# Part A's last projection chunk with high and low weights in one array, and a new split of the maxima over the projection products

## The chip, the cores and the metric

The kernel runs on one core of one Trainium2 chip. The metric is the device time of one execution in microseconds; lower is better. The core's engines work side by side, each through its own list of instructions in order, and wait for each other through semaphores: TensorE (PE, with its weight loads as PEld), VectorE (DVE), ScalarE (ACT), GpSimd (POOL), and SyncE (SP), which here only issues DMA transfers.

## What is computed

Two attention blocks over x of 2048 rows and 576 columns, 32 heads of 18. Part A is local and dilated, part B is full. Their outputs stand side by side.

```python
# part A
qkv = (x @ wqkv).reshape(B, S, 3, H, Dh)...
idx = pos[:, None] - off[None, :]          # 8 keys, 2 apart
kg = k[:, :, idx_c, :]; vg = v[:, :, idx_c, :]
attn = softmax(where(mask, einsum("bhsd,bhswd->bhsw", q, kg) * scale, -1e9))
a = einsum("bhsw,bhswd->bhsd", attn, vg)... @ wo
# part B
scores = einsum("bhqd,bhkd->bhqk", q, k) * scale
b = einsum("bhqk,bhkd->bhqd", softmax(scores), v)... @ wo
return concatenate([a, b], axis=-1)
```

## The kernel before

Every float32 operand of a projection is split into a high part (rounded to TensorE's fp32r) and a low part (the rest), and a product is the sum of three: high by high, high by low, low by high. The 576 input rows are four pieces of 128 and a last one of 64, whose high and low parts of x share one tile (`xhl`) on the two halves of the partitions, so that it takes two passes in place of three.

**Start.** Three chunks of part B's q and k (`w0`) and half of its values are projected with full 128-row passes.

**The stream** (function `stream`, passes recorded at L491) follows: 96 products in groups of four. A product is cut into two halves by rows of the weights' contraction: half 0 on partitions 0 to 63, half 1 on 64 to 127, which run side by side on the array. A turn j takes half 0 of one product and half 1 of another, so that a group takes four turns and both halves of a product add up in the same PSUM bank; 13 or 14 passes a half, 27 a product (`halves`, with the triples from `pairs`). The products are 16 of the other values (288 columns wide), 24 of part B's q and k (`w1`, `w2`) and 56 of part A: 14 chunks of its 1728 columns, 13 of 128 columns and the last, number 13, of 64, each for four blocks of 512 rows of x. In a group, product k has bank k of the ring "scores" (banks 0 to 3).

Among the passes stand **maxima** of part B's scores: `maximum(r)` multiplies 128 queries with 512 keys on half r (L239) into one of three banks (ring "else", banks 4 to 6), and DVE reduces it (L256, L258). A pair is one on each half. The function handed to `stream` as `most` says how many pairs have been given by each turn; by the end it is `EARLY_PAIRS`, 264. The last turn also holds the four scores of the first step of the main loop (`others`; L388), which ACT turns into exponentials (L398).

After the third and the fourth turn of a group its products are emptied (`leave_a` for part A): ACT copies a bank into one of the four buffers `ohi` (L819), and SP stores it to the array `da` in DRAM (L820). The product that stands second in number is copied first. In the 64-column chunk the copy and the store have 64 partitions.

The weights of a part A chunk come in `chunk`: `put` and `put_last` have ACT make the high part and POOL the low part (L538, L539), as tiles `ahi`, `alo` (four pieces) and `ahh`, `all` (the last piece). `a_room` deals the chunks out to pools in turn, one buffer each.

**The main loop** has 511 steps over 8 groups of heads, 4 blocks of queries and 16 of keys: four scores, their exponentials, products with v (L870), and the maxima of blocks two groups ahead; part A's local attention runs on POOL beside it from step 10 on, and reads `da`: q and k before, v 16 steps later. Its first step begins with half of a two-part maximum in bank 0, a score in bank 1 and a whole maximum in bank 2 (`PLAIN`, "D1AzwE2B"); the pair tile for `z` and `w` is banks 5 and 6, and the score `2` goes to bank 3.

Nothing reorders the work at run time: the order of every engine is what the program records, and the functions above set it.

Of the kernel before, what the change touches and what calls it, by code (L numbers as in the profile page):

```python
# [23 lines left out]
NT = S // 128  # L24
# [16 lines left out]
EARLY_PAIRS = EARLY * NB * PIECES + 8  # L41
# [28 lines left out]
def two_attentions(ctx: ExitStack, tc, xa, wa, woa, xb, wb, wob, out):  # L70
# [5 lines left out]
    nc = tc.nc  # L76
# [354 lines left out]
    def halves(r, odd, w, x, wcols, xcols, weights_move=False):  # L431

        at = slice(64 * r, 64 * r + 64)
        both = [p for c in range(4) for p in pairs(c, w, x, wcols, xcols)] + pairs(4, w, x, wcols, xcols)[: 1 + (r == odd)]
        return [(b[at], a[at]) if weights_move else (a[at], b[at]) for a, b in both]


    ctx.enter_context(tc.manual_schedule())
    make_set(stack0, 0)
# [11 lines left out]
    def stream(products, most, last):  # L451

        where, ends = {}, {}  # L460
        for j in range(len(products)):
            first = j - j % 4
            turn = [((0, 0), (1, 1)), ((0, 2), (1, 3)), ((0, 1), (1, 0)), ((0, 3), (1, 2))][j % 4]
            both = []
            for r, k in turn:
                args, view, _ = products[first + k]
                if j % 4 < 2:
                    where[k] = view(bank("scores"))
                else:
                    assert int(sum(given)) - ends[k] > 3  # L470
                parts = halves(r, *args)
                both.append([(where[k], *ab, j % 4 < 2 and i == 0, j % 4 > 1 and i == len(parts) - 1)
                             for i, ab in enumerate(parts)])
            n = most(j) - given[0]
            others = last if j == len(products) - 1 else ([], [])
            n += len(others[0])
            total = n + len(both[0])
            for r in range(2):
                for i in range(n):
                    both[r].insert((4 * i + 1 + 2 * r) * total // (4 * n), None)  # L480
            narrow = where[turn[0][1]].shape[-1] < 512
            spent = [0, 0]
            while any(both):
                r = int(not both[0] or bool(both[1]) and spent[1] < spent[0])
                p = both[r].pop(0)
                spent[r] += 133 if p and narrow else 226
                if p is None:
                    (others[r].pop(0) if others[r] else maximum(r))()
                else:
                    ps, a, b, start, stop = p  # L490
                    nc.tensor.matmul(ps, a, b, start=start, stop=stop)  # L491
            for _, k in turn:
                if j % 4 < 2:
                    ends[k] = int(sum(given))
                else:
                    products[first + k][2](where[k])
            slot()
# [5 lines left out]
    every = slice(0, 512)  # L503
# [4 lines left out]
    with (tc.tile_pool(name="x", bufs=1, side="right") as xp,  # L508
# [28 lines left out]
        def split(engine, hi, lo, t):  # L537
            nc.scalar.activation(hi, t, AF.Copy)  # L538
            engine.tensor_sub(lo, t, hi)  # L539
# [38 lines left out]
        def chunk(c):  # L578

            n = min(128, 3 * D - 128 * c)  # L580
            t = {}
            w = [None] * 4

            def get():
                t[0] = rp.tile([128, 512], F32, name="raw", bufs=5)
                load(ap(t[0], (n, 4), (1, n)), rows(wa[0, 128 * c], (3 * D, 128), (128 * 3 * D, 4), (1, n)))

            def get_last():
                t[1] = rp.tile([128, 512], F32, name="raw", bufs=5)
                for r in range(2):  # L590
                    load(t[1][64 * r : 64 * r + 64, :n], wa[512:, 128 * c : 128 * c + n])

            def put():
                hi, lo = (a_room(c).tile([128, 512], F32R, name=nm, bufs=1) for nm in ("ahi", "alo"))
                split(nc.gpsimd, hi[:, : 4 * n], lo[:, : 4 * n], t[0][:, : 4 * n])
                w[:2] = ([u[:, n * k : n * k + n] for k in range(4)] for u in (hi, lo))

            def put_last():
                w[2:] = (a_room(c).tile([128, 128], F32R, name=nm, bufs=1) for nm in ("ahh", "all"))
                split(nc.gpsimd, w[2][:, :n], w[3][:, :n], t[1][:, :n])  # L600

            return w, [get, get_last], [put, put_last]

        def a_room(c):
            return a0 if c % 2 == 0 else a1 if c == 1 else wp


        qkv, odd = ExitStack(), ExitStack()
# [3 lines left out]
        if True:  # L612
# [34 lines left out]
            for c in range(5):  # L647
                one, other = (load, nc.scalar.dma_start) if c % 2 == 0 else (nc.scalar.dma_start, load)
# [9 lines left out]
            x = [t[0] for t in xs]  # L658
# [69 lines left out]
            for t in range(NT):  # L728
                ps = bank()
# [10 lines left out]
            xas = [inputs(xa, b, nc.gpsimd, spare="more" if b == NB - 1 else False) for b in range(NB)]  # L740
            w1, w1_get, w1_put = weights(proj[1], wb, turn_cols(1), nc.vector)
            w2, w2_get, w2_put = weights(proj[0], wb, turn_cols(2), nc.gpsimd)
            ws = [chunk(c) for c in range(14)]

            def second_rows():

# [61 lines left out]
            for k in range(2, 14):  # L808
                n = 46 if k == 2 else 36 + 4 * k
# [6 lines left out]

            def leave_a(c, b, n, ps):
                o = xp.tile([128, 512], F32, name="ohi", bufs=4)
                nc.scalar.activation(o[:n], ps, AF.Copy)  # L819
                load(da[128 * c : 128 * c + n, HALO + 512 * b : HALO + 512 * b + 512], o[:n])  # L820


            order = [t for i in (0, 8) for j in range(4) for t in (i + j, i + j + 4)]
            ring = "else"
            nc.vector.memset(po, 0.0)
            work_list = []
# [12 lines left out]
            for c, b in order:  # L839
                n = min(128, 3 * D - 128 * c)  # L840
                work_list.append(((b % 2, ws[c][0], xas[b][0], slice(0, n), every),
                                  lambda ps, n=n: ps[:n], lambda ps, c=c, b=b, n=n: leave_a(c, b, n, ps)))

            es = []
            few = 6 * NT // 4
            turns = len(work_list) - NT
            stream(work_list, lambda j: 6 * (j // 4) + (1, 3, 5, 6)[j % 4] if j < NT else
                   few + (EARLY_PAIRS - few) * (j - NT + 1) // turns,
                   [[lambda h=h: es.append(score(0, 0, 0, h, "apart" if h in (1, 2) else "single")) for h in (r, r + 2)] for r in range(2)])
        wa_room.close()  # L850

# [304 lines left out]
    turns = []  # L1156
# [200 lines left out]
    while step < ALL:  # L1357
        n, kt = divmod(step, NT)
        g, b = divmod(n, NB)
# [4 lines left out]
        products = inside.pop(0)() if inside else ([], [])  # L1364
# [3 lines left out]
        parts = many == 3 or many == 1 and open_parts  # L1368
# [75 lines left out]
```

## Time and profile before

| | us |
|---|---|
| median of 3 runs | 1590.14 |
| lowest, highest | 1588.71, 1592.66 |
| profiled execution, its own time | 1589.66 |
| its span, first to last instruction | 1587.8 |
| value products of the stream | 74.6 to 109.7 |
| part B's other products of the stream | 109.7 to 201.3 |
| part A's products, 128 columns | 201.3 to 400.5 |
| part A's products, 64 columns | 400.5 to 417 |
| main loop's first wait on the stream is over | 418.5 |

The profile is one execution seen by the hardware profiler. A row of the timeline has the start in us from the span's start, the time it covers, engine, line, operation, the tile written and those read, the shape (rows\*columns of the weights for a pass, then what is streamed) and a count; in brackets the engine's idle time before it and what ended that. A row of a group has the count, busy us and mean ns of one, and the idle time before. A pass of 64 rows lasts some 390 ns from its start to its modelled end, but passes overlap, so what a pass costs is read from the starts of those that follow.

### The profile page before, as it was taken

What the parts mean: (1) busy time and instruction counts of PE and PEld (TensorE: products, weight loads), DVE (VectorE), ACT (ScalarE), POOL (GpSimd) and SP (SyncE); (2) the same over time, 40 slices, a digit from 0 to 9 for tenths busy, and PEclk for the clock granted to TensorE, in tenths of its full rate; (3) what the DMA queues carried; (4) which work ended last, traced back from release to release, by engine and by line L of the source; (5) the groups of instructions that cost most, each with busy time, mean ns of one, the idle gap of its engine ahead of it and who ended that gap; (6) DMA issues with size and microseconds to landing.
All of it is one profiled execution on the core that took longest, in us unless ns stands there. A gap on an engine that the chain in (4) does not pass through costs nothing.

```text
span 1587.8 us, 34762 instructions
## 1 busy us (share of the span) xinstructions
PE 1577.4 (99%) x13436; PEld 971.1 (61%) x13436; DVE 1399.7 (88%) x2381; ACT 1180.6 (74%) x1912; POOL 961.6 (61%) x816
## 2 busy tenths in 40 slices
PE   9999999999999999999999999999999999999998
PEld 7999999999544444444444445444445445455776
DVE  5299999999999999999998999999999999999433
ACT  6324441121699999999998999999999999998444
POOL 2305752201157997994994995995995997940100
PEclk9999999999999999999999999999999999999999
DMA  9848954532322253253236225324613232234211
GB/s 258 222 142 207 274 171 124 146 98 76 75 52 58 63 115 90 69 127 113 60 83 167 52 76 134 104 50 107 143 53 91 70 87 78 61 125 157 85 39 60
DMA packets 190149, 173.12 MB, mean 109 GB/s; under 512 B 123120, under 2 KB 136944, under 8 KB 188256
## 3 DMA queue, kind: packets, MB, share of 16 engines
q1 hardware_dynamic: 185120, 159.36, 36.1%
q0 software_dynamic: 4032, 10.63, 3.2%
q8 instruction: 105, 1.72, 0.5%
q10 hardware_dynamic: 832, 0.92, 0.2%
q14 instruction: 60, 0.49, 0.1%
HBM read 97.47 MB, written 72.95 MB: 107 GB/s over the span
## 4 chain that ended last, share of the span: by engine, by line
PE 97%; DVE 2%; DMA 1%; issue 0%; ACT 0%; POOL 0%; SPq 0%; ACTq 0%; DVEq 0%; POOLq 0%
PE po L870 31%; PE bank L239 20%; PE bank L491 17%; PE bank L388 10%; PE bank L1211 8%; PE pair L388 7%; PE bank L424 4%; DVE mx L256 1%; DMA at<-dao 0%; DVE mx L272 0%; DVE o L880 0%; PE bank L643 0%; DVE mx L258 0%; DMA out<-y 0%; PE bank L1189 0%
## 5 line engine op out<-in xcount | busy, mean ns | idle before, releaser
L239 PE MATMUL bank<-ks,qs 54*128 54x256 f32 (+1 forms) x2526 | 754.6, 372 | 1.0 <-ACT ohi L819 0.9
L256 DVE TENSOR_REDUCE mx<-bank 128x1 f32<-128x512 f32 x1024 | 680.1, 684 | 63.8 <-PE bank L239 39.6
L239 PEld LDWEIGHTS bank<-ks,qs 54*128 54x128 f32 x2526 | 414.2, 184 | 424.3 <-DVE mx L272 305.0
L398 ACT ACTIVATE e<-bank 128x512 f32<-128x512 f32 x1024 | 610.1, 602 | 71.5 <-PE bank L388 64.4
L870 PE MATMUL po<-ee,v 128*19 128x512 f32 x2048 | 537.1, 599 | 1.0 <-DVE o L880 0.2
L870 PE MATMUL po<-e,v 128*19 128x512 f32 x2048 | 531.8, 599 | 0.0
L401 ACT ACTIVATE ee<-pair 128x1024 f32<-128x1024 f32 x478 | 487.2, 1019 | 0.9 <-PE pair L388 0.3
L388 PE MATMUL bank<-qs,ks 56*128 56x512 f32 x1092 | 461.0, 442 | 0.0
L258 DVE TENSOR_REDUCE mx<-bank 128x2 f32<-128x512 f32 x546 | 356.5, 684 | 19.5 <-PE bank L239 6.6
L272 DVE TENSOR_REDUCE mx<-bank 128x2 f32<-128x512 f32 x478 | 326.1, 682 | 0.0
L388 PE MATMUL pair<-qs,ks 56*128 56x512 f32 x956 | 248.7, 396 | 0.0
L388 PEld LDWEIGHTS bank<-qs,ks 56*128 56x128 f32 x1092 | 194.6, 184 | 15.9 <-ACT e L398 9.0
L1062 POOL TENSOR_TENSOR pr<-lg,akv 128x1024 f32<-128x1024 f32 x72 | 157.0, 2200 | 0.6
L819 ACT ACTIVATE ohi<-bank 128x512 f32<-128x512 f32 (+1 forms) x56 | 30.4, 595 | 156.4 <-issue 129.1
L388 PEld LDWEIGHTS pair<-qs,ks 56*128 56x128 f32 x956 | 138.1, 185 | 0.1
L870 PEld LDWEIGHTS po<-ee,v 128*19 128x19 f32 x2048 | 69.6, 96 | 112.0 <-issue 108.1
L491 PE MATMUL bank<-xhi,ahi 64*128 64x512 f32 (+1 forms) x448 | 120.2, 390 | 0.0
L491 PE MATMUL bank<-xhi,alo 64*128 64x512 f32 (+1 forms) x448 | 114.5, 390 | 0.0
L491 PE MATMUL bank<-xlo,ahi 64*128 64x512 f32 (+1 forms) x448 | 108.8, 391 | 0.1
L1014 POOL TENSOR_TENSOR pr<-aq,akv 128x1024 f32<-128x1024 f32 x40 | 87.8, 2202 | 18.3 <-PE bank L239 17.1
L1064 POOL TENSOR_TENSOR pr<-pr 128x512 f32<-128x512 f32 x72 | 91.1, 1285 | 0.6
L539 POOL TENSOR_TENSOR alo<-raw,ahi 128x512 fp32r<-128x512 f32 (+1 forms) x14 | 17.6, 1257 | 117.4 <-ACT ahi L538 86.0
(206 smaller groups left out, 2383.7 us busy)
## 6 DMA issues: line engine op xcount, KB each, us to landing
do<-n SPq DMA_DIRECT2D x28, 512.0 KB
da<-ohi SPq DMA_DIRECT2D x52, 256.0 KB
akv<-da SPq DMA_DIRECT2D x64, 175.5 KB
out<-y SPq DMA_DIRECT2D x32, 288.0 KB
qs<-dqk SPq DMA_DIRECT2D x30, 288.0 KB
ks<-dqk SPq DMA_DIRECT2D x30, 288.0 KB
at<-dao SPq DMA_DIRECT2D x64, 128.0 KB
rec<-drec SPq DMA_DIRECT2D x29, 256.0 KB
```

The lines of the kernel that those rows point to most:

```text
L239: return nc.tensor.matmul(ps, qs[rows_, b, p, 128 * t : 128 * t + 128], ks[rows_, p, 512 * k + at : 512 * k + at + n], start=True, stop=True)
L256: nc.vector.tensor_reduce(mx[:, r, p, t, k : k + 1], ps, axis=AX.X, op=ALU.max)
L258: nc.vector.tensor_reduce(mx[:, r, p, t, 2 * k - 2 : 2 * k], ps.rearrange("q (h n) -> q h n", h=2), axis=AX.X, op=ALU.max)
L272: nc.vector.tensor_reduce(mx[:, :, p, t, 2 * k - 2 + i], ps.rearrange("q (h n) -> q h n", h=2), axis=AX.X, op=ALU.max)
L388: nc.tensor.matmul(ps, ks[at, p, 128 * kt : 128 * kt + 128], qs[at, b, p], start=True, stop=True)
L398: nc.scalar.activation(e, ps, AF.Exp, scale=SCALE)
L401: nc.scalar.activation(whole, both_scores[0], AF.Exp, scale=SCALE)
L491: nc.tensor.matmul(ps, a, b, start=start, stop=stop)
L870: nc.tensor.matmul(po[32 * i : 32 * i + 19], vs[g][:, kt, 19 * i : 19 * i + 19], es[i], start=kt == 0, stop=kt == NT - 1)
L1062: nc.gpsimd.tensor_mul(at, ap(st["lg"], (0, 2), (SUB, W), (1, SUB)), window(st["v"], n))
L1064: nc.gpsimd.tensor_add(at[:, :, :4], at[:, :, :4], at[:, :, 4:])
L1211: nc.tensor.matmul(sums_[r], a, b, start=i == 0, stop=i == len(both[r]) - 1)
```

## The change

The weights of the 64-column chunk are laid out with high and low part side by side, 64 columns each, in one tile: a pass with all 128 columns against the high part of x gives high by high in partitions 0 to 63 of the bank and low by high in 64 to 127; a second pass with the first 64 columns against the low part of x adds high by low in 0 to 63. That makes two passes a piece and one for the last, 9 a half, 18 a product (`joined`). `leave_a` then copies both halves of the bank and POOL adds them before the store.

The chunk moves from the last place to the last but one (`turn_of`), so that the stream ends with the 128-column chunk 12. `most` becomes a table: the value products get 7 pairs in a group of four where they had 6, the 64-column products 2 each where they had 3, all others 3 as before; the total stays 264. Two of the four early scores go to the last turn but one. And the two products that end in a turn are copied in the order of their numbers.

```diff
+    def joined(r, odd, w, x):
+
+        at = slice(64 * r, 64 * r + 64)
+        xhi, xlo, xhl = x
+        both = [p for c in range(4) for p in ((w[c][at], xhi[c][at]), (w[c][at, :64], xlo[c][at]))]
+        return both[:6] + [(w[4][at] if r == odd else w[4][at, :64], xhl[at])] + both[:5:-1]
...
-                parts = halves(r, *args)
-                both.append([(where[k], *ab, j % 4 < 2 and i == 0, j % 4 > 1 and i == len(parts) - 1)
+                parts = (joined if len(args) == 3 else halves)(r, *args)
+                both.append([(where[k][: ab[0].shape[1]], *ab, j % 4 < 2 and i == 0, j % 4 > 1 and i == len(parts) - 1)
...
-            others = last if j == len(products) - 1 else ([], [])
+            others = [o[:1] for o in last] if j == len(products) - 2 else [o[1:] for o in last] if j == len(products) - 1 else ([], [])
...
-            for _, k in turn:
+            for k in sorted(k for _, k in turn):
...
             def put():
+                if n == 64:
+                    both = a_room(c).tile([128, 4, 2, 64], F32R, name="ahi", bufs=1)
+                    one = t[0][:, :256].rearrange("p (k n) -> p k n", k=4)
+                    split(nc.gpsimd, both[:, :, 0], both[:, :, 1], one)
+                    w[:] = [both[:, k].rearrange("p i n -> p (i n)") for k in range(4)]
+                    return
...
             def put_last():
+                if n == 64:
+                    last = a_room(c).tile([128, 128], F32R, name="ahh", bufs=1)
+                    split(nc.gpsimd, last[:, :64], last[:, 64:], t[1][:, :64])
+                    w.append(last)
+                    return
...
+        turn_of = [*range(12), 13, 12]
+
         def a_room(c):
+            c = turn_of[c]
...
-            ws = [chunk(c) for c in range(14)]
+            ws = [chunk(c) for c in turn_of]
...
             def leave_a(c, b, n, ps):
                 o = xp.tile([128, 512], F32, name="ohi", bufs=4)
-                nc.scalar.activation(o[:n], ps, AF.Copy)
+                nc.scalar.activation(o[:n], ps[:n], AF.Copy)
+                if n == 64:
+                    lo = xp.tile([128, 512], F32, name="ohi", bufs=4)
+                    nc.scalar.activation(lo[:n], ps[n:], AF.Copy)
+                    nc.gpsimd.tensor_add(o[:n], o[:n], lo[:n])
                 load(da[128 * c : 128 * c + n, HALO + 512 * b : HALO + 512 * b + 512], o[:n])
...
-            few = 6 * NT // 4
-            turns = len(work_list) - NT
-            stream(work_list, lambda j: 6 * (j // 4) + (1, 3, 5, 6)[j % 4] if j < NT else
-                   few + (EARLY_PAIRS - few) * (j - NT + 1) // turns,
+            most = []
+            for j, (args, _, _) in enumerate(work_list):
+                most.append((most or [0])[-1] + {6: (1, 2, 2, 2), 5: (3, 3, 3, 3), 3: (2, 2, 2, 2)}[len(args)][j % 4])
+            assert most[-1] == EARLY_PAIRS
+            stream(work_list, lambda j: most[j],
```

Three places in the order of the engines show it. The first is PE at the start of the 64-column group. L491 (before) and L498 (now) are the stream's passes, written as bank<-x,weights with the shape of the result; L239 is a maximum. Before:

```order
L491 MATMUL bank_5878<-xhi,ahi 64x512
L491 MATMUL bank_5879<-xhi,ahi 64x512
L239 MATMUL bank_5882<-ks_1585,qs_1584 128x512
L491 MATMUL bank_5879<-xlo,ahi 64x512
L491 MATMUL bank_5878<-xlo,ahi 64x512
L491 MATMUL bank_5879<-xhi,alo 64x512
L491 MATMUL bank_5878<-xhi,alo 64x512
```

Now:

```order
L498 MATMUL bank_5690<-xhi,ahi 128x512
L498 MATMUL bank_5691<-xhi,ahi 128x512
L239 MATMUL bank_5694<-ks_1609,qs_1608 128x512
L498 MATMUL bank_5691<-xlo,ahi 64x512
L498 MATMUL bank_5690<-xlo,ahi 64x512
L498 MATMUL bank_5691<-xhi,ahi 128x512
L498 MATMUL bank_5690<-xhi,ahi 128x512
```

Where a piece took the passes xhi,ahi, xlo,ahi and xhi,alo on each half, it now takes one of 128 and one of 64 columns, and the next piece follows.

The second is ACT at the end of the stream: `ohi` rows empty banks (L819 before, L840 and L843 now), L398 and L401 are exponentials of the early scores and of the main loop's first step. Before:

```order
L819 ACTIVATE ohi_6020<-bank1_5879 64x512
L819 ACTIVATE ohi_6023<-bank0_5878 64x512
L398 ACTIVATE e00_6030<-bank4_6028 128x512
L398 ACTIVATE ee0_6038<-bank5_6036 128x512
L398 ACTIVATE ee0_6038<-bank6_6042 128x512
L398 ACTIVATE e10_6051<-bank4_6049 128x512
L819 ACTIVATE ohi_6087<-bank3_5927 64x512
L819 ACTIVATE ohi_6090<-bank2_5926 64x512
L398 ACTIVATE e01_6112<-bank1_6110 128x512
```

Now:

```order
L840 ACTIVATE ohi_5846<-bank3_5729 64x512
L843 ACTIVATE ohi_5848<-bank3_5729 64x512
L398 ACTIVATE e00_5954<-bank4_5952 128x512
L398 ACTIVATE ee0_5962<-bank5_5960 128x512
L840 ACTIVATE ohi_6002<-bank0_5852 128x512
L840 ACTIVATE ohi_6005<-bank1_5853 128x512
L398 ACTIVATE ee0_5962<-bank6_6012 128x512
L398 ACTIVATE e10_6021<-bank4_6019 128x512
L840 ACTIVATE ohi_6061<-bank2_5900 128x512
L840 ACTIVATE ohi_6064<-bank3_5901 128x512
L398 ACTIVATE e01_6086<-bank1_6084 128x512
```

Two exponentials now stand ahead of the last group's first copies, directly behind the doubled copies of the 64-column group, and bank 2 is emptied ahead of bank 3.

The third is DVE in the value products, where subtractions (`wlo`) stand between the reductions (`mx`). Before:

```order
L256 TENSOR_REDUCE mx<-bank_1187 128x1
L256 TENSOR_REDUCE mx<-bank_1197 128x1
L539 TENSOR_TENSOR wlo<-raw,whi 128x384
L256 TENSOR_REDUCE mx<-bank_1217 128x1
L256 TENSOR_REDUCE mx<-bank_1233 128x1
L539 TENSOR_TENSOR wlo<-raw,whi 128x384
```

Now:

```order
L546 TENSOR_TENSOR wlo<-raw,whi 128x384
L256 TENSOR_REDUCE mx<-bank_1219 128x1
L256 TENSOR_REDUCE mx<-bank_1229 128x1
L256 TENSOR_REDUCE mx<-bank_1239 128x1
L256 TENSOR_REDUCE mx<-bank_1249 128x1
L546 TENSOR_TENSOR wlo<-raw,whi 128x384
```

Between two subtractions in the third group of value products stand four reductions where there were two.

More of the change, by code (lines that the diff above doesn't have):

```diff
@@ L838, in two_attentions @@
             order += [(c, b) for c in range(2, 14) for b in range(NB)]
-            for c, b in order:
+            for k, b in order:
+                c = turn_of[k]
                 n = min(128, 3 * D - 128 * c)
-                work_list.append(((b % 2, ws[c][0], xas[b][0], slice(0, n), every),
-                                  lambda ps, n=n: ps[:n], lambda ps, c=c, b=b, n=n: leave_a(c, b, n, ps)))
+                args = (b % 2, ws[k][0], xas[b][0])
+                work_list.append((args if n == 64 else (*args, slice(0, n), every),
+                                  lambda ps: ps, lambda ps, c=c, b=b, n=n: leave_a(c, b, n, ps)))
             es = []
-            few = 6 * NT // 4
-            turns = len(work_list) - NT
-            stream(work_list, lambda j: 6 * (j // 4) + (1, 3, 5, 6)[j % 4] if j < NT else
-                   few + (EARLY_PAIRS - few) * (j - NT + 1) // turns,
+            most = []
[3 more added lines that the diff above has]
+            stream(work_list, lambda j: most[j],
                    [[lambda h=h: es.append(score(0, 0, 0, h, "apart" if h in (1, 2) else "single")) for h in (r, r + 2)] for r in range(2)])
```

## The prediction

> **What bounds the kernel now.** I read the page first: engine shares and the chain of waits.
>
> ```profile
> span 1587.8 us, 34762 instructions
> PE 1577.4 (99%) x13436; PEld 971.1 (61%) x13436; DVE 1399.7 (88%) x2381; ACT 1180.6 (74%) x1912; POOL 961.6 (61%) x816
> PE 97%; DVE 2%; DMA 1%; issue 0%; ACT 0%; POOL 0%; SPq 0%; ACTq 0%; DVEq 0%; POOLq 0%
> ```
>
> TensorE carries 97% of the chain that ends last. DVE's 88% is an average over a first stage without maxima and a last one with few, so I cut the span into the stages that the change touches: the value products, the other Part B products, the Part A products, the end of the stream and the main loop. Columns: stretch, its length, then busy us and instructions of PE, PEld, DVE, ACT, POOL, the granted clock, DMA share, GB/s.
>
> ```profile
> 74.60:109.70 35.10, 34.98 (x480) 34.43 (x481) 31.49 (x53) 8.62 (x35) 0.54 (x2) 1.00 0.41 129
> 109.70:201.30 91.60, 91.60 (x797) 91.60 (x795) 90.15 (x148) 36.96 (x69) 56.51 (x57) 1.00 0.87 243
> 201.30:402.00 200.70, 200.60 (x1733) 188.86 (x1731) 195.96 (x325) 46.91 (x92) 45.61 (x59) 1.00 0.41 121
> 400.50:418.50 18.00, 17.18 (x141) 11.81 (x137) 15.90 (x28) 5.18 (x11) 0.47 (x2) 1.00 0.15 45
> 418.50:1587.80 1169.30, 1161.46 (x9912) 582.39 (x9912) 1038.80 (x1796) 1041.82 (x1613) 833.55 (x663) 1.00 0.34 89
> ```
>
> In the Part A stretch 1733 passes take 200.70 us: **0.116 us a pass**, and PE has no idle time. A wide product has 27 passes and 6 maxima, 33 x 0.116 = 3.83 us. DVE is close behind, 97.6% busy. What a reduction costs DVE is read where several stand back to back:
>
> ```profile
> 409.36 3.69 DVE L256 TENSOR_REDUCE mx<-bank 128x1 f32<-128x512 f32 x6
> 415.01 3.68 DVE L256 TENSOR_REDUCE mx<-bank 128x1 f32<-128x512 f32 x6 [1.83 <-PE bank L239]
> L258 DVE TENSOR_REDUCE mx<-bank 128x2 f32<-128x512 f32 x16 | 10.0, 684 | 1.0 <-PE bank L239 0.8
> ```
>
> One lasts 0.68 us, six in a row 3.69: the next starts (3.69 - 0.68) / 5 = **0.60 us** after the last. Six make 3.6 us against PE's 3.83. So PE sets the pace by 6%; time taken off PE is gained only where maxima leave with it, and a product that gets more maxima is soon DVE's.
>
> **The change, part by part.** All sums are made against the profiled execution, 1589.66 us (span 1587.8 and 1.9 around it); the median of the runs is 1590.14, 0.5 above it.
>
> 1. *The 64-column products.* Four products drop from 27 passes to 18 and from 6 maxima to 4: 4 x (9 + 2) = 44 passes leave. The new pass has 128 columns of weights where the old had 64; the trace has both kinds side by side:
>
> ```profile
> 410.45 0.39 PE L491 MATMUL bank<-xlo,ahi 64*64 64x512 f32 x2
> 410.68 0.39 PE L491 MATMUL bank<-xhi,alo 64*64 64x512 f32 x1
> 410.69 0.39 PE L239 MATMUL bank<-ks,qs 54*128 54x512 f32 x1
> 410.92 0.39 PE L491 MATMUL bank<-xhi,ahi 64*64 64x512 f32 x1
> ```
>
> Pairs start 0.23 us apart whether they hold 64 or 128 columns or one of each, so the time goes by streamed columns (512 in all) and 0.116 holds: 44 x 0.116 = **-5.1 us**. What is left, 22 passes, is 2.55 us a product; DVE needs 4 x 0.60 = 2.4. DVE hardly holds it back. The joint weight array has as many elements as before, so its split on ACT and POOL costs nothing new, and it moves with its products, keeping their lead.
>
> 2. *Four pairs of maxima go to the value products.* There 24 pairs become 28. On PE that is 8 x 0.116 = +0.9 us, the lower bound. On DVE it is 8 x 0.60 = 4.8 us, the upper bound if DVE had no slack. Between them decide the groups of four products, seen by the copies that empty their banks, and the weight subtractions that DVE does among them:
>
> ```profile
> 81.52 0.84 ACT L709 ACTIVATE vs<-bank 128x144 f32<-128x144 f32 x4 [6.32 <-PE bank L491]
> 90.41 0.84 ACT L709 ACTIVATE vs<-bank 128x144 f32<-128x144 f32 x4 [3.23 <-PE bank L491]
> 99.51 0.84 ACT L709 ACTIVATE vs<-bank 128x144 f32<-128x144 f32 x4 [5.49 <-PE bank L491]
> 108.06 0.84 ACT L709 ACTIVATE vs<-bank 128x144 f32<-128x144 f32 x4 [5.76 <-PE bank L491]
> 85.77 0.55 DVE L539 TENSOR_TENSOR wlo<-raw,whi 128x384 fp32r<-128x384 f32 x1
> 86.24 2.48 DVE L256 TENSOR_REDUCE mx<-bank 128x1 f32<-128x512 f32 x4
> ```
>
> The groups take 8.89, 9.10 and 8.55 us; two subtractions fall in the first of these and three in the second, each 0.47 us of DVE (85.77 to 86.24). A group without them is PE's: 8.55, with seven pairs 8.55 + 2 x 0.116 = 8.8. With seven pairs DVE needs 14 x 0.60 = 8.4, with two subtractions 9.3, with three 9.8: these two groups become DVE's. The sum is 8.8 + 9.3 + 9.8 + 8.8 = 36.7 against 35.1, and three products in four now have 2.4 us of reductions for about 2.3 of passes, worth a few tenths more since only three banks hold maxima. I take **+2.0 us**.
>
> 3. *Emptying the 64-column products.* Each now takes two copies, an add on POOL and two of the four store buffers. ACT and POOL are idle for three quarters of the Part A stretch, so the work itself (4 more copies, 4 adds) is hidden; the order on ACT is not. Rows, for ACT's start at 0:
>
> ```profile
> 400.80 1.09 ACT L819 ACTIVATE ohi<-bank 128x512 f32<-128x512 f32 x2 [2.61 <-PE bank L239]
> 122.93 2.55 POOL L631 TENSOR_TENSOR olo<-olo,ohi 128x512 fp32r<-128x512 f32 x2 [9.60 <-ACT ohi L630]
> L574 POOL TENSOR_TENSOR xhl<-raw,xhl 64x512 fp32r<-64x512 f32 x3 | 3.9, 1295 | 0.2
> 412.99 1.14 SPq L820 DMA_DIRECT2D da<-ohi  x2
> 415.00:415.50 0.50, 0.50 (x5) 0.26 (x5) 0.49 (x1) 0.38 (x1) 0.00 (x0) 1.00 0.77 160
> 415.50:416.00 0.50, 0.50 (x6) 0.38 (x7) 0.50 (x2) 0.00 (x0) 0.00 (x0) 1.00 0.01 0
> ```
>
> The copies of products 0 and 1 run to 2.1, the two adds to 2.5 and 3.75, the stores are issued at 2.55 and 3.8. Two such stores issued from 412.99 had moved all bytes by 415.5, so a store lands about 2.0 after its issue (estimate): 4.6 and 5.8. Of the next two products, the third and fourth copies take the buffers that these stores free, so the last copy runs 5.9 to 6.5. PE's first pass into that bank comes two turns on: it starts 0.3 before ACT's copies, then 2.55 and 3.83 pass, 6.1. It waits **+0.5 us**, all passes behind it too; bounds 0 and +0.9 (a landing of 1.5 or 2.4).
>
> 4. *Two scores a turn sooner, wide products last, first copy first.* The rows of the end:
>
> ```profile
> 400.49 0.40 PE L491 MATMUL bank<-xhi,ahi 64*64 64x512 f32 x1
> 412.06 0.39 PE L388 MATMUL bank<-qs,ks 56*128 56x512 f32 x1
> 412.38 1.07 ACT L819 ACTIVATE ohi<-bank 64x512 f32<-64x512 f32 x2 [10.49 <-issue]
> 413.82 1.07 ACT L398 ACTIVATE ee<-bank 128x512 f32<-128x512 f32 x2
> 416.93 0.39 PE L491 MATMUL bank<-xhl,ahh 64*64 64x512 f32 x1
> 417.41 1.07 ACT L819 ACTIVATE ohi<-bank 64x512 f32<-64x512 f32 x2 [2.03 <-issue]
> 418.54 0.50 PE L239 MATMUL bank<-ks,qs 54*128 54x512 f32 x1 [0.85 <-ACT ohi L819]
> ```
>
> From 400.49 to 418.54 stand 4 x 33 passes, 4 scores and 2 passes of the main loop: 138 x 0.116 = 16.0 of 18.05 us, so 2.05 are waits. Some 0.9 arise because four scores take the three banks of the maxima while ACT still copies (DVE idles 1.83 before 415.01); the other 1.1 at the seam (416.93 to 418.54 less four passes), where the main loop's maximum needs bank 2, emptied by the second of two copies. Afterwards two scores come in a turn in which ACT is free, and two behind 1.09 us of copies: about 0.4 stays. At the seam bank 2 is emptied first, 0.5 sooner. I take **-1.0 us**; bounds 0 and -2.05. In the other groups the swapped copies cost nothing: nobody needs those banks for a whole turn, 3.83 us against 1.09.
>
> 5. *The main loop* keeps its passes, maxima and stores; the wide chunk stored last belongs to the values of Part A, read only some 26 steps on. It starts sooner and I let it run its 1169.3 us.
>
> Sum: -5.1 + 2.0 + 0.5 - 1.0 = **-3.6**: 1586.1 from the profiled execution, 1586.5 from the median. I say **1586.3**. That is 0.23% under the median; 0.3%, 4.8 us, is about what a measurement of this kernel can tell from no change, so the likeliest single verdict is "same" with a real small gain under it.
>
> **Rivals.** *The whole gain.* DVE lets the value products go at PE's price (+0.9), the stores land early (0), and 1.6 of the 2.05 us at the end go: -5.8, about 1584.1. For it: DVE has 3.6 us free there now. Against: nearly all its free time lies in the groups without subtractions.
>
> *DVE takes it back.* The value products pay the whole 4.8 us: -0.8, about 1589.1. For it: the groups with subtractions already take 8.89 and 9.10 us, 0.3 and 0.5 over the PE-bound one, though DVE's work in them sums to 12 x 0.60 + 0.94 = 8.1 and 8.6; against: the last group leaves DVE 8.55 - 7.2 = 1.35 us.
>
> *The store buffers hold PE.* Part 3 alone can turn the sign. ACT runs in order: while its last copy waits for a landing, the exponentials behind it wait, and PE's pass into that bank stops everything. The wait is the landing time less 1.5 us, so with 4.1 us of wait, a landing of 5.6, the gain is gone. At 7.5 us, the median of the loads that POOL issues, it is 6.0: -3.6 + 5.5 = +1.9, about 1591.8.
>
> ```profile
> qs<-dqk POOLq DMA_DIRECT2D x18, 288.0 KB, 7.5
> ```
>
> Against: that row is another queue with other shapes, and the stores of these very tiles moved within 2.5.
>
> The Trainium skill, page "TensorEngine Tiling (Array Packing)", section "PSUM Bottleneck", speaks for this rival: array tiling speeds up TensorE but not the emptying of PSUM, which may then become the bound. By that rule the time would be this rival's, not the sum's; no run here has yet shown a product that needs two copies and an add.
>
> **How the numbers follow.** Forecast 0.49, whole gain 0.30, DVE takes it back 0.14, store buffers 0.07. Faster by over 0.3% means under 1585.4: most of the second case (0.28) and the edge of the first (0.08), 0.36. Slower by over 0.3% means over 1594.9: only the last case, with DVE's 4.8 us on top or a landing beyond 10 us, 0.03. Same: 0.61. The best bounds together give -5.1 + 0.9 - 2.05 = -6.3, the worst of parts 2 to 4 give -5.1 + 4.8 + 0.9 = +0.6: 1583.4 to 1590.6, which leaves out the last rival and a main loop that runs otherwise.
>
> **What would show it.** The value products take 36.5 to 38 us instead of 35.1, with DVE over 95% busy there; their middle groups 9.3 or more. The four 64-column products start 2.55 us apart, not 3.83. ACT's last copy of the second pair ends about 6.5 us after the first copy of the first pair, and PE shows a gap of at most 1 us two turns on. DVE's 1.83 us gap is gone, and the main loop begins about 3.6 us sooner and takes 1169 us. I am wrong if pairs with 128 and 64 columns of weights start further apart than 0.23 us, if the value products grow by more than 3 us, or if the main loop's length moves by more than 2 us.

## The result and the profile after

The changed kernel takes 1585.6 us (median of 12 runs, 1583.38 to 1587.25) against 1589.73 us for the kernel before (12 runs, 1587.52 to 1593.07). The ratio is 0.9971 with a 95% interval of 0.9962 to 0.9980: a gain of 0.3%, 4.1 us by the medians, clear of no change and just at the edge of the 0.3% that was called measurable. The forecast was 3.6 us less than before, 1586.3.

The page of the changed kernel's profiled execution (1584.54 us):

```profile
span 1582.7 us, 34698 instructions
PE 1571.9 (99%) x13400; PEld 949.5 (60%) x13400; DVE 1399.5 (88%) x2381; ACT 1183.0 (75%) x1916; POOL 966.0 (61%) x820
PE 93%; DVE 2%; DMA 2%; issue 1%; POOL 1%; ACT 1%; SPq 0%; POOLq 0%; ACTq 0%; DVEq 0%
```

There are 36 passes fewer, 4 copies and 4 adds more, and PE is still what ends last. The stages, in the columns of the first windows above; the cuts are the first passes of the value products, of the other Part B products, of Part A, of the 64-column chunk, of the last wide chunk, and of what the main loop waited for:

```profile
74.30:111.90 37.60, 36.90 (x490) 35.89 (x490) 35.33 (x60) 8.50 (x35) 0.54 (x2) 1.00 0.39 120
111.90:203.60 91.70, 91.70 (x797) 91.65 (x795) 90.80 (x151) 37.41 (x69) 56.55 (x57) 1.00 0.86 239
203.60:387.80 184.20, 184.04 (x1589) 156.51 (x1588) 179.84 (x299) 42.51 (x84) 43.73 (x57) 1.00 0.43 126
387.80:398.00 10.20, 10.19 (x88) 7.46 (x84) 9.95 (x17) 4.29 (x8) 2.91 (x3) 1.00 0.23 76
398.00:415.60 17.60, 16.97 (x137) 13.28 (x137) 15.68 (x27) 6.25 (x12) 4.38 (x6) 1.00 0.22 61
415.60:1582.70 1167.10, 1159.28 (x9912) 581.61 (x9912) 1039.02 (x1796) 1042.08 (x1614) 832.98 (x663) 1.00 0.34 89
```

The value products grew from 35.1 to 37.6 us, Part B's others did not move, and the four 64-column products take 10.2 us, where the four took 15.3 by the old count of passes. To see what is the change and what is the execution, both kernels were profiled once more (labels r_before and r_after). From first pass to first pass, in us; "stream" ends at the main loop's first product with v (L870 before, L898 now):

| | before | again | changed | again |
|---|---|---|---|---|
| value products | 35.20 | 35.95 | 37.58 | 37.42 |
| other Part B products | 91.68 | 91.68 | 91.69 | 91.68 |
| Part A up to the seam | 217.92 | 217.93 | 212.97 | 212.91 |
| stream in all | 344.81 | 345.57 | 342.24 | 342.02 |
| main loop to the end | 1168.37 | 1166.60 | 1166.17 | 1167.29 |

The stream repeats within 0.25 us but for one wait: in the second execution of before the first maximum came 0.66 us late (a gap of 0.78 where starts usually lie 0.12 apart), and without it its value products take 35.3. So **the stream gained 2.7 us**, 5.0 in Part A less 2.3 in the value products. The main loop, whose program is the same in both, differs by 1.8 us between two executions of one kernel.

### The profile page after: what moved, and what is told of

It is laid out like the page before. It is cut to its first block, busy times and chain, and to the rows that moved or that the text cites. A ratio compares the mean times of both kernels' runs of the same rounds, so it can differ in the third digit from the quotient of the medians.

```text
span 1582.7 us, 34698 instructions
## 1 busy us (share of the span) xinstructions
PE 1571.9 (99%) x13400; PEld 949.5 (60%) x13400; DVE 1399.5 (88%) x2381; ACT 1183.0 (75%) x1916; POOL 966.0 (61%) x820
## 4 chain that ended last, share of the span: by engine, by line
PE 93%; DVE 2%; DMA 2%; issue 1%; POOL 1%; ACT 1%; SPq 0%; POOLq 0%; ACTq 0%; DVEq 0%
PE po L898 30%; PE bank L239 20%; PE bank L498 14%; PE bank L388 9%; PE bank L1239 8%; PE pair L388 7%; PE bank L424 4%; DVE mx L256 1%; DMA ks<-dqk 1%; POOL xlo L546 1%; DMA qs<-dqk 0%; DMA at<-dao 0%; DVE mx L272 0%; DVE o L908 0%; PE bank L664 0%
## 5 line engine op out<-in xcount | busy, mean ns | idle before, releaser
L239 PE MATMUL bank<-ks,qs 54*128 54x256 f32 (+1 forms) x2526 | 756.1, 373 | 1.2 <-DVE mx L256 0.5
L239 PEld LDWEIGHTS bank<-ks,qs 54*128 54x128 f32 x2526 | 414.9, 184 | 427.5 <-DVE mx L272 308.3
L398 ACT ACTIVATE e<-bank 128x512 f32<-128x512 f32 x1024 | 610.9, 602 | 75.5 <-PE bank L388 68.6
L898 PE MATMUL po<-ee,v 128*19 128x512 f32 x2048 | 536.9, 599 | 1.0 <-DVE o L908 0.2
L898 PE MATMUL po<-e,v 128*19 128x512 f32 x2048 | 531.5, 599 | 0.0
L401 ACT ACTIVATE ee<-pair 128x1024 f32<-128x1024 f32 x478 | 487.5, 1020 | 0.3
L840 ACT ACTIVATE ohi<-bank 128x512 f32<-128x512 f32 (+1 forms) x56 | 30.6, 595 | 148.6 <-issue 126.3
L898 PEld LDWEIGHTS po<-ee,v 128*19 128x19 f32 x2048 | 69.8, 97 | 111.3 <-issue 107.4
L498 PE MATMUL bank<-xhi,ahi 64*128 64x512 f32 x448 | 114.6, 391 | 0.2 <-ACT ohi L843 0.2
L498 PE MATMUL bank<-xlo,ahi 64*128 64x512 f32 (+1 forms) x448 | 102.7, 392 | 0.2 <-POOL xlo L546 0.2
L498 PE MATMUL bank<-xhi,alo 64*128 64x512 f32 x416 | 101.0, 391 | 0.0
L652 POOL TENSOR_TENSOR olo<-olo,ohi 128x512 fp32r<-128x512 f32 x36 | 46.1, 1294 | 65.7 <-ACT ohi L651 61.3
```

What stands on the lines that cost most here:

```text
L239: return nc.tensor.matmul(ps, qs[rows_, b, p, 128 * t : 128 * t + 128], ks[rows_, p, 512 * k + at : 512 * k + at + n], start=True, stop=True)
L398: nc.scalar.activation(e, ps, AF.Exp, scale=SCALE)
L401: nc.scalar.activation(whole, both_scores[0], AF.Exp, scale=SCALE)
L898: nc.tensor.matmul(po[32 * i : 32 * i + 19], vs[g][:, kt, 19 * i : 19 * i + 19], es[i], start=kt == 0, stop=kt == NT - 1)
```

## The experiments

All but the last two are single executions with a profile, and are read by the lengths of their stages, not by their total time.

**r_before and r_after: the two kernels unchanged.** No edit.

> The kernel before, unchanged, once more, to learn how much its stages differ between executions. If the stages repeat, the value products take 35.2 us again, the stream from its first pass to the main loop's first product with v 344.8, and the main loop 1168.4. If the main loop was the accident (it was 2.2 us shorter in the changed kernel's profile, 1.3 of it in one place near 855 us), it moves here by one or two microseconds and the stream does not.

> The changed kernel, unchanged, once more. Theory (the change works in the stream alone): value products 37.6 us, stream 342.2, and a main loop anywhere between 1166 and 1168.5. Rival (the main loop gains too): the main loop again 2 us under that of the kernel before, and again by a step near 855 us.

Measured: the table above. The main loop of before was 1.8 us shorter this time, that of the changed kernel 1.1 longer. Most of what differs between two executions of one kernel lies in a single place, steps 180 to 220 (a step is counted by its eight products with v), which took 90.7 and 88.8 us before and 89.5 and 90.3 after. Of the 2.2 us between the main loops of the first two profiles 1.2 lie there. The rest of the loop repeats: it took 1077.7 and 1077.8 us before, 1076.7 and 1077.0 now.

**e_old_table: the old split of the maxima.**

```diff
-{6: (1, 2, 2, 2), 5: (3, 3, 3, 3), 3: (2, 2, 2, 2)}
+{6: (1, 2, 2, 1), 5: (3, 3, 3, 3), 3: (3, 3, 3, 3)}
```

> The changed kernel with the old split of the maxima: 6 pairs in a group of value products, 3 pairs in each 64-column product. Theory (DVE sets the pace of a product that has too many maxima): the value products return to 35.2 us; the 64-column products, 24 passes or 2.8 us of PE, have 6 reductions of 0.60 and start 3.6 us apart instead of 2.55, so that the four take about 14.4 instead of 10.2 us; sum against the changed kernel +1.8. Rival (PE alone sets the pace, DVE's backlog is carried on): the four take 11.1, sum -1.5.

The value products took 36.95, of which 1.55 is the late first maximum again: 35.4. The 64-column products started 3.00, 3.59, 3.58 and 3.60 apart, 13.8 us in all. DVE's timeline there shows why:

```profile
387.60 15.03 DVE L258 TENSOR_REDUCE mx<-bank 128x2 f32<-128x512 f32 x25
```

Twenty-five reductions in an unbroken row, (15.03 - 0.68) / 24 = 0.60 us apart. A product of 24 passes (18 and 6 maxima) has 2.8 us for PE and takes the 3.6 of its six reductions; only the first is shorter, which fits a lag of DVE by the maxima that the banks hold. PE alone would have made 11.1 of the four: the rival falls. The whole from the chunk's first pass to the main loop was 32.1 us against 29.15, +2.9, less than +3.6: the slower products also gave the copies and stores time, and ACT's waits on the store buffers fell from 2.0 us to 0.8. With the value products' -2.1 that is +0.8 for the old table; +1.8 was expected.

**e_old_passes: the old layout of the 64-column chunk.** All else as in the changed kernel, two pairs of maxima a product included; the first edit stands at all three places that ask for 64 columns.

```diff
-                if n == 64:
+                if False:
...
-                args if n == 64 else (*args, slice(0, n), every)
+                (*args, slice(0, n), every)
```

> The changed kernel with the 64-column chunk in its old layout: three passes a piece, one copy, no add; place in the order, maxima table, scores and copy order stay new. Theory (time goes by passes, at 0.116 us): 31 passes instead of 22 a product, the four start 3.60 instead of 2.55 us apart, +4.2, and the waits on the store buffers and the doubled copies go, -0.6; stream 342.1 + 3.6 = 345.7. Rival (a pass with 128 columns of weights saves less than it replaces): the difference is under 2.5.

Four products took 14.4 us, 3.60 apart on average, against 10.22, and from the chunk's first pass to the main loop 32.67 against 29.15: +3.5, as expected (+3.6). The stream was 346.3, of which some 0.5 is a late first maximum. The joint weights are worth this much, net of the longer emptying.

**e_spread: the four pairs elsewhere.**

```diff
-{6: (1, 2, 2, 2), 5: (3, 3, 3, 3), 3: (2, 2, 2, 2)}[len(args)][j % 4])
+{6: (1, 2, 2, 1), 5: (3, 3, 3, 3), 3: (2, 2, 2, 2)}[len(args)][j % 4] + (j in (44, 54, 64, 74)))
```

> The changed kernel with the four moved pairs of maxima not in the value products but one each in four wide products of part A, ten turns apart. Theory (DVE lags by what the three banks hold and catches up at 0.23 us a product): value products 35.2 us, each of the four wide products longer by 2 passes, 0.23 us, sum against the changed kernel -2.4 + 0.9 = -1.5. Rival (a product with 8 reductions waits for DVE at once): each longer by 8 x 0.60 - 3.83 = 1.0 us, sum +1.5.

Value products 35.30, Part A's wide products +1.75 (185.55 against 183.80): 0.44 us for each of the four pairs, between the 0.23 of PE and the 1.0 of DVE. That is a mean: the first falls into a turn that takes 4.4 us with or without it and costs nothing, the others cost 0.7, 0.4 and 0.6 with the turns behind them. Stream 341.7, 0.4 less than the changed kernel's, where -1.5 was expected and +1.5 by the rival: better than the value products, hardly so.

**e_pool_sub: the weight subtractions of the value products on POOL.**

```diff
-w1, w1_get, w1_put = weights(proj[1], wb, turn_cols(1), nc.vector)
+w1, w1_get, w1_put = weights(proj[1], wb, turn_cols(1), nc.gpsimd)
```

> The changed kernel with the five weight subtractions among the value products on POOL instead of DVE. Theory (the two groups with subtractions are DVE's, the others PE's): value products 37.6 - 1.5 to 2.0 = 35.6 to 36.1 us, four groups of about 8.8 to 9.0. Rival (the added maxima cost their full time whoever subtracts, by waits in each product): value products stay above 37.

The copies that empty the groups (timeline of ACT), first in the changed kernel, then with POOL subtracting:

```profile
81.38 0.84 ACT L730 ACTIVATE vs<-bank 128x144 f32<-128x144 f32 x4 [6.49 <-PE bank L498]
90.60 0.84 ACT L730 ACTIVATE vs<-bank 128x144 f32<-128x144 f32 x4 [3.79 <-PE bank L498]
100.97 0.84 ACT L730 ACTIVATE vs<-bank 128x144 f32<-128x144 f32 x4 [5.56 <-PE bank L498]
109.96 0.84 ACT L730 ACTIVATE vs<-bank 128x144 f32<-128x144 f32 x4 [5.76 <-PE bank L498]
```

```profile
81.61 0.84 ACT L730 ACTIVATE vs<-bank 128x144 f32<-128x144 f32 x4 [6.33 <-PE bank L498]
90.41 0.84 ACT L730 ACTIVATE vs<-bank 128x144 f32<-128x144 f32 x4 [3.10 <-PE bank L498]
99.21 0.84 ACT L730 ACTIVATE vs<-bank 128x144 f32<-128x144 f32 x4 [4.94 <-PE bank L498]
108.00 0.84 ACT L730 ACTIVATE vs<-bank 128x144 f32<-128x144 f32 x4 [5.76 <-PE bank L498]
```

With DVE subtracting the groups take 9.22, 10.37 and 8.99 us; with POOL 8.80, 8.80 and 8.79, the 8.8 that the prediction summed for a group that is PE's with seven pairs. The stage is back at 35.28, no longer than before the change. So 2.2 of the 2.3 us hang on the five subtractions, 5 x 0.47 = 2.35 us of DVE, most of which before had fitted in beside six pairs.

**e_five_bufs: a fifth store buffer.**

```diff
-xp.tile([128, 512], F32, name="ohi", bufs=4)
+xp.tile([128, 512], F32, name="ohi", bufs=5)
```

The same number is changed wherever `ohi` is made, in Part B's emptying too.

> The changed kernel with five store buffers instead of four. Theory (the last copy of the 64-column chunk waits for the landing of a store): that copy starts about 5.0 us after the first instead of 6.3, and the 0.57 us gap on PE two turns on shrinks to the usual 0.12 to 0.23; the stream gets 0.3 to 0.5 us shorter. Rival (the gap has another cause, POOL's add or the order on ACT): it stays.

ACT's copies of the four 64-column products (the first two of the eight, then the last four) and PE two turns on, in the changed kernel:

```profile
395.52 0.59 ACT L840 ACTIVATE ohi<-bank 64x512 f32<-64x512 f32 x1 [5.35 <-issue]
396.13 0.59 ACT L843 ACTIVATE ohi<-bank 64x512 f32<-64x512 f32 x1
398.13 0.59 ACT L840 ACTIVATE ohi<-bank 64x512 f32<-64x512 f32 x1 [0.16 <-POOL ohi L844]
399.38 0.59 ACT L843 ACTIVATE ohi<-bank 64x512 f32<-64x512 f32 x1 [0.66 <-POOL ohi L844]
400.40 0.59 ACT L840 ACTIVATE ohi<-bank 64x512 f32<-64x512 f32 x1 [0.43 <-DMA da<-ohi]
401.78 0.59 ACT L843 ACTIVATE ohi<-bank 64x512 f32<-64x512 f32 x1 [0.78 <-DMA da<-ohi]
401.85 0.39 PE L498 MATMUL bank<-xhi,ahi 64*128 64x512 f32 x1
402.42 0.49 PE L498 MATMUL bank<-xhi,ahi 64*128 64x512 f32 x1 [0.19 <-ACT ohi L843]
```

And the first and the last copy and PE at the same place with five buffers:

```profile
395.83 0.59 ACT L840 ACTIVATE ohi<-bank 64x512 f32<-64x512 f32 x1 [5.35 <-issue]
400.72 0.60 ACT L843 ACTIVATE ohi<-bank 64x512 f32<-64x512 f32 x1 [0.45 <-DMA da<-ohi]
402.14 0.39 PE L498 MATMUL bank<-xhi,ahi 64*128 64x512 f32 x1
402.38 0.39 PE L498 MATMUL bank<-xhi,ahi 64*128 64x512 f32 x1
```

With four buffers the last copy starts 6.26 us after the first (395.52 to 401.78) and PE's pass into that bank follows it at 402.42, 0.57 after its partner. With five it starts 4.89 after (395.83 to 400.72), and the partners are 0.24 apart. From the chunk's first pass to the main loop it is 28.72 us instead of 29.15: the store buffers cost 0.43. The waits for POOL's add, which also frees a buffer, go with them.

**e_late_scores: four scores in the last turn.**

```diff
-others = [o[:1] for o in last] if j == len(products) - 2 else [o[1:] for o in last] if j == len(products) - 1 else ([], [])
+others = last if j == len(products) - 1 else ([], [])
```

> The changed kernel with all four early scores in the last turn again. Theory (four scores take the maxima's three banks while ACT copies): DVE idles about 1.8 us in the last turn and the stream gets about 0.5 us longer or more. Rival (the gain at the end came from the wide chunk standing last): no change of the stream beyond 0.2 us.

DVE in the last two turns, first with the four scores together, then as changed:

```profile
408.86 3.70 DVE L256 TENSOR_REDUCE mx<-bank 128x1 f32<-128x512 f32 x6
414.75 4.28 DVE L256 TENSOR_REDUCE mx<-bank 128x1 f32<-128x512 f32 x7 [2.07 <-PE bank L239]
```

```profile
407.87 3.74 DVE L256 TENSOR_REDUCE mx<-bank 128x1 f32<-128x512 f32 x6 [0.58 <-PE bank L239]
412.19 3.75 DVE L256 TENSOR_REDUCE mx<-bank 128x1 f32<-128x512 f32 x6 [0.47 <-PE bank L239]
```

One wait of 2.07 us against two of about 0.5. From the 64-column chunk to the main loop 29.82 against 29.15: the earlier scores are worth 0.67 us. The stream in all, 344.55, is 2.4 longer, but 1.1 of that is a late first maximum and 0.4 one longer turn in Part B's products.

**e_old_order: the second product copied first.**

```diff
-            for k in sorted(k for _, k in turn):
+            for _, k in turn:
```

> The changed kernel with the second product copied first, as before. Theory (the main loop's maximum waits for bank 2): the gap at the seam grows from 0.85 to about 1.25 us, the stream by 0.4 to 0.5. Rival (another wait lies just behind, so the order is worth nothing): under 0.1.

The seam, with the old order and then as changed:

```profile
414.32 0.39 PE L388 MATMUL bank<-qs,ks 56*128 56x512 f32 x1
415.60 0.50 PE L239 MATMUL bank<-ks,qs 54*128 54x512 f32 x1 [0.89 <-ACT ohi L840]
```

```profile
414.78 0.39 PE L388 MATMUL bank<-qs,ks 56*128 56x512 f32 x1
415.63 0.50 PE L239 MATMUL bank<-ks,qs 54*128 54x512 f32 x1 [0.46 <-ACT ohi L840]
```

1.28 us against 0.85, the 0.43 of one copy. The stretch as a whole is only 0.22 longer (29.37 against 29.15): PE's first passes after the 64-column group, which as changed wait for bank 1 (starts 0.42 apart near 398.0), are held up less with the old order: the second pair starts 0.78 us after the last pass of that group (397.35 to 398.13), as changed 0.99 (397.36 to 398.35). The theory holds at its place, and the same edit gives half of it back elsewhere.

**e_both: subtractions on POOL and five buffers**, five rounds beside the kernel before.

> The changed kernel with the weight subtractions on POOL and five store buffers. Theory (the two terms lie in different stages and add up): value products 35.3 us, stream 342.1 - 1.9 - 0.4 = 339.8, time 1583.3 and 6.4 under the kernel before. Rival (one gives back what the other saves): stream above 340.5.

1583.43 us (five runs, 1581.48 to 1587.81) against 1590.44 for before: ratio 0.9952, interval 0.9939 to 0.9966. In its profile the end of the stream takes 28.71 us as with five buffers alone; the value products took 37.99, of which 2.65 is a late first maximum, so 35.3: the two terms add up. The stream itself was 342.2 in this execution, above the rival's 340.5, but by that one wait and not by a term given back.

**e_both_early: the same, with the loads of the local part's output up to six steps sooner.**

```diff
-            pieces.append((max(at + 1, one - 9) - start, lambda n=n: get(n)))
+            pieces.append((max(at + 1, one - 15) - start, lambda n=n: get(n)))
```

> The same with the loads of the local part's output (tile at) up to six steps sooner in the main loop. Theory (the 0.9 to 2.6 us in which PE waits for this load near step 205, and the lower clock that follows some of these waits, make the main loop's length differ between executions): steps 180 to 220 take 88 us or less, in every execution, instead of 88.8 to 93.1, time 1 to 4 us less, 1580 to 1582, and the spread of the runs shrinks. Rival (the load is late since the transfers ahead of it in SP's queue are): the wait stays, no change of time.

1581.40 us (five runs, 1579.59 to 1584.45), ratio to before 0.9946, interval 0.9934 to 0.9958. The list of waits between 836 and 866 us in the changed kernel (second execution; total us, times, longest):

```profile
PE bank L1239 <- DMA at<-dao: 2.5, 2, 2.1
```

The window around the place, for that kernel and then for this one:

```profile
846.00:856.00 10.00, 7.46 (x70) 4.05 (x69) 7.33 (x16) 5.20 (x10) 0.71 (x1) 1.00 0.60 163
```

```profile
846.00:856.00 10.00, 10.00 (x106) 7.03 (x106) 10.00 (x21) 6.51 (x12) 1.70 (x3) 1.00 0.57 196
```

The wait is gone, and steps 180 to 220 take 87.3 us, the shortest of all 13 profiles. The medians of e_both and e_both_early differ by 2.0 us, but their intervals overlap; what is shown is that the wait went. Against the changed kernel, with its ratio of 0.9962 to 0.9980, only the interval of e_both_early lies clear of it: its median is the lowest found. The five runs spread over 4.9 us, those of e_both over 6.3; that the spread shrinks is not shown, and the steps were read in the one profiled execution.

## Why the prediction was right, point by point

**What bounds it.** That PE sets the pace and DVE follows within 6% is shown from both sides: a 64-column product with 18 passes and 4 maxima takes 2.56 us (2.55 predicted), PE's price; with 18 passes and 6 maxima 3.6, DVE's.

**Term 1, -5.1.** Four products took 10.22 us against the 4 x 3.83 of before. Alone, and net of what it brings with it, the layout is worth 3.5 (e_old_passes). A pass with 128 columns of weights costs what one with 64 does, shown in the mixed products themselves:

```profile
390.39 0.40 PE L498 MATMUL bank<-xlo,ahi 64*64 64x512 f32 x2
390.61 0.41 PE L498 MATMUL bank<-xhi,ahi 64*128 64x512 f32 x2
390.84 0.42 PE L498 MATMUL bank<-xlo,ahi 64*64 64x512 f32 x2
```

Pairs of 64 and of 128 columns follow each other at 0.22 to 0.23 us.

**Term 2, +2.0; measured +2.2 to +2.4.** The mechanism and the place were right: the groups with subtractions became DVE's. They took 9.22 and 10.37 us where 9.3 and 9.8 were summed, with DVE busy for 94% of the stage, just under the 95 that were named. The group with three subtractions lost 0.6 more, and 0.4 of that is a wait that the sum had not: twice a subtraction stands on DVE 0.20 us for the high part of its weights, which ACT makes only behind copies that wait for PE; reductions queue behind it, and PE waits for one of them.

```profile
91.30 0.55 ACT L545 ACTIVATE whi<-raw 128x384 fp32r<-128x384 f32 x1
91.87 0.56 DVE L546 TENSOR_TENSOR wlo<-raw,whi 128x384 fp32r<-128x384 f32 x1 [0.20 <-ACT whi L545]
93.09 0.49 PE L239 MATMUL bank<-ks,qs 54*128 54x512 f32 x1 [0.47 <-DVE mx L256]
94.45 0.55 ACT L545 ACTIVATE whi<-raw 128x384 fp32r<-128x384 f32 x1
95.03 0.56 DVE L546 TENSOR_TENSOR wlo<-raw,whi 128x384 fp32r<-128x384 f32 x1 [0.20 <-ACT whi L545]
```

The second execution has the same two waits, 0.21 each. The lower bound, +0.9 by PE, was set against the whole stage as it stood and so was too high: of the 35.2 us before, 1.0 were already DVE's (4 x 8.55 is 34.2), and with POOL subtracting the stage with all four pairs takes 35.28, no more than before.

**Term 3, +0.5; measured 0.43.** The last copy started 6.26 us after the first, 5.9 predicted: copies one after another start 0.62 apart where 0.50 was read from a row of other copies, and the stores took 2.3 to 2.4 us (398.12 to 400.40, and 399.37 to 401.78) where 2.0 was estimated. The 0.4 us come from the reuse of a buffer and go with one buffer more; by the time of the copies themselves the emptying costs the 0.3 of the wait on bank 1, under term 4. The rule of the Trainium skill ("TensorEngine Tiling (Array Packing)", "PSUM Bottleneck"), that copies out of PSUM may become the bound, thus shows in this small wait alone. As a rival, the store buffers were far from turning the sign.

**Term 4, -1.0; measured -0.74.** Taken back one at a time the parts are worth 0.67 (scores) and 0.22 (order, net of what it gives back), but set against the kernel before they overlap. The four turns of the last group (the starts of their first passes, the last turn up to the first product with v) took 3.9, 3.7, 4.0 and 7.3 us before and 4.2, 4.2, 4.2 and 6.4 now, in both executions of each within 0.1. The last two turns, with the scores and the seam, fell from 11.29 to 10.55. The second turn grew by the 0.4 of term 3. The first grew by 0.3: the new copies brought one wait that was not seen. PE's first passes after the 64-column group want bank 1 before the chunk's first four copies, of 2.45 us against a turn of 2.56, are through; with five buffers this turn is as long.

**The sum.** -3.6 was forecast for the stream, -2.7 came. The error is 0.3 in term 2 and the rest in Part A, whose -5.0 falls 0.6 short of the three terms' -5.6: 0.3 of it is the wait on bank 1, and most of the rest the 0.26 that term 4 missed.

**The main loop, 0.** Its program did not change, and as a whole its length did not follow the kernel: 1168.4 and 1166.6 for before, 1166.2 and 1167.3 for the changed one. The first pair differs by 2.2 us, a little more than the 2 that the prediction named as a sign of being wrong; the means differ by 0.75. Outside steps 180 to 220, though, the loop is 0.7 to 1.1 us shorter in both executions of the changed kernel than in both of before, and this the forecast had at nothing. The other versions, with one profile each, take 1076.9 to 1077.8 us there, so it is not the change as such. Steps 119, 236, 439 and 467 last 2.2 us in both executions of before and 2.0 in all eleven of the changed versions; step 90 of the changed kernel goes the other way. In each of these long steps ACT stands idle for 0.09 to 0.10 us ahead of one exponential, and the weight load of a score waits 0.16 to 0.17 for ACT; in the short ones neither shows. Why ACT stands there, and in which steps, stays open.

The medians of 12 runs say 4.1 us with an interval of some 3.2 to 6.0. The stream gives 2.7 of it and this part of the main loop 0.9 by the means; what is left may be chance. So the total came out within 0.5 us of the forecast in part by luck: the stream fell 0.9 short, and the main loop made up for it.

**Rivals.** The whole gain failed on DVE in the value products; "DVE takes it back" paid 2.3 of the 4.8 us; the store buffers 0.4 of the 4.1 that they would have needed.

## What to carry to other kernels

Where two engines run within a few per cent of each other, passes taken from the first are worth little unless the second's work leaves that place too (the four products fell from 15.3 us to 13.8 with their old maxima, to 10.2 with four fewer pairs), and moved work is priced where it lands: the four pairs cost 2.3 us beside five subtractions, and with these on an idle engine the stage took no longer than before. Count the engine's other work in each group of the destination, and what that work waits for, not its mean over the stage. A copy that now takes two buffers and an add should get a buffer more before its time is worried about.

## What the hardware showed that was not expected

A part of the spread of the profiles can be pinned to a place. Near 850 us PE waits for a load of the local part's output, 0.5 to 2.6 us over the profiles (the 0.5 follows a wait of 1.0 that is put down to ACT), and in seven of the twelve profiles that have the wait the granted clock drops to half, between 0.1 us before the end of its longest wait there and 1.8 after. The same 16 us in three of them (columns as before, the clock third from the end): r_after, without a drop,

```profile
844.00:860.00 16.00, 13.46 (x130) 8.13 (x127) 13.33 (x26) 9.55 (x18) 2.98 (x4) 1.00 0.64 175
```

e_both, with one,

```profile
844.00:860.00 16.00, 13.37 (x108) 8.37 (x106) 11.82 (x25) 9.59 (x17) 2.33 (x4) 0.89 0.62 167
```

and e_five_bufs, with a larger one:

```profile
844.00:860.00 16.00, 13.43 (x95) 7.39 (x93) 10.52 (x22) 8.42 (x14) 1.34 (x2) 0.79 0.56 145
```

Their waits are nearly the same (2.5, 2.6 and 2.6 us), and steps 180 to 220 take 90.3, 91.8 and 93.1 us. The clock missing is 0.11 x 16 = 1.8 and 0.21 x 16 = 3.4 us: one and two times the same amount. The stretches themselves, in e_both and in e_five_bufs:

```profile
851.49:854.90 3.41, 3.35 (x26) 3.38 (x28) 1.05 (x2) 0.00 (x0) 0.00 (x0) 0.50 0.80 285
850.48:857.31 6.83, 6.45 (x39) 4.28 (x39) 1.84 (x3) 1.50 (x3) 0.00 (x0) 0.50 0.57 189
```

Half speed lasts 3.41 us in five profiles and 6.83 in two. The Trainium skill, page "TensorE: Matmul & The Clock Gate", section "What's actually happening", says that the gate knows full and half speed, and decides in windows of some 3.4 us that run on regardless of the program. One and two such windows at half speed miss 1.7 and 3.4 us (an estimate from the figures of this page of the Trainium skill), which agrees with these rows. The traces also place the windows: in each, the changes of the clock lie whole multiples of 3.413 us apart, as 853.66 and 1587.52 in the first profile of before (733.86 = 215 x 3.4133). In e_both the long wait, 848.5 to 850.7, lies whole in the window from 848.1 to 851.5, at whose end the drop starts; in r_after, whose clock falls at 1583.24 when the run ends, a boundary at 849.4 cuts the wait from 847.8 to 849.9 in two, and no drop follows. That nearly equal waits end in different clocks fits this. It is not the whole rule: r_after has 1.6 us of waiting in one window and no drop, e_old_table 1.2 us and a drop. This page of the Trainium skill has the drop after an idle window; here drops began after windows with 1.2 to 2.6 us of waiting.

Also not expected: the first maximum of the stream comes late, by up to 2.7 us, in some of the executions, one of before included. The profile names no releaser for it, and it was not followed up.
